# Pacing a spectral transform beside a feed-forward block: two straight lines for the transform's steps, and maxima of x taken five steps behind their loads

## The chip, the cores and the metric

The kernel runs on one core of one Trainium2 chip. The metric is the device time of one execution in microseconds (us), lower is better. The profile names the engines PE (TensorE, matmuls; PEld is its weight load), DVE (VectorE), ACT (ScalarE), POOL (GpSimd) and SP (SyncE, whose queue issues all DMA transfers here; SPq is that queue).

## The reference

For 8 batches of 3136 tokens with 256 channels: a filter in the frequency domain along the tokens, then a two-dimensional Fourier transform whose real part is added, a normalization over the channels, and a feed-forward block with 1024 hidden channels.

```python
X = np.fft.rfft(x, axis=1)
x = np.fft.irfft(X * (filt_r + 1j * filt_i)[None], n=3136, axis=1)
mixed = np.real(np.fft.fft(np.fft.fft(x, axis=1), axis=2))
u = x + mixed
mu = np.mean(u, axis=-1, keepdims=True)
var = np.mean((u - mu) ** 2, axis=-1, keepdims=True)
un = (u - mu) / np.sqrt(var + 1e-06)
out = u + np.maximum(un @ w_ch1, 0.0) @ w_ch2
```

## The kernel before

All matrix products run in float16, with each operand split into a high and a low part, so three matmuls stand for one. Two kinds of work share the engines.

**The transform of a batch, there and back.** `there(b)` is a generator; each `yield` ends one *step*, and a batch has `STEPS` = 63 of them.

- Stage 1 (`forward1`): seven loads of x (448 KB each, L379, tile `x`), one a step; `XLAG` steps behind each load the maximum of that tile on VectorE (`absmax`, L267, tile `mx`); then a scale `sx` from the seven maxima; then 14 steps, each with a cast on ScalarE and a subtraction on VectorE (L395), three matmuls (L400), an eviction by ScalarE and VectorE (L402, L403) and a store into the DRAM tile `d1` (224 KB, L404).
- Stage 2 (`forward2`): seven chunks. Each loads `at` from `d1` (L425), forms the spectrum (L449, L450), multiplies it by the filter on VectorE (L455, L459), finishes it on GpSimd, ScalarE and GpSimd or VectorE, and turns it around by a transposing DMA (`z`, L480). Two chunks later `inverse1` multiplies `z` (L514 to L516) and stores `bt` into the DRAM tile `d2` (L520). `fold` writes the chunk's even and odd parts into the ring `eo` of 1920 columns, from which the channel mix reads.
- The way back (`inverse2`, generator `back(b)`, 17 *back steps*): it loads `b` from `d2` (448 KB, L554; all chunks of `d2` have to be there), waits two more steps, forms y (L577), evicts it on ScalarE (`ys`, L584) and stores it into the DRAM tile `dy` (L560). The first back step of a batch holds its first b load, the fourth its first y product.

The generators begin a batch's transform when the one before is through its last step; a back step may come once all but the last step of its batch's transform are done.

**The feed-forward block.** Tokens go in 49 groups of 256 mirrored pairs of rows (two tiles of 128; 1568 pairs a batch, so group 6 holds the first pairs of batch 1, and groups 12, 18, 24, 30, 36 and 42 the first of batches 2 to 7). `fetch(g)` loads y from `dy` (L633); `prepare(g)` yields seven times: two channel mixes (L646, reading `eo`), the add on VectorE (L656), the statistics (L713, L714), the scale (L725 to L729), and two tiles that are normalized (L736), split (L739, L741) and turned around by a transposing DMA (`ut`, L746). Then the group has eight *products*: `first_product(g, f)` is six matmuls (L770) with an eviction in two halves (`h`: ScalarE L779, VectorE L780), and `second_product`, two products behind, is twelve matmuls into `acc` (L799). After the eighth, `acc` is added to y (L808) and stored (L811). 392 products make up the run.

**Pacing.** The main loop goes over the products q. In each it emits a first product, one yield of a group's preparation (group g+2 begins at f = 2 of group g), a second product, at most one back step, and then as many transform steps as a pacing line says. At f = 6 of group g, group g+3 is fetched, and `bring` emits at once whatever back steps its rows still need. For the first group with rows of batch 2 to 7 this is at q = 78, 126, 174, 222, 270 and 318. `advance` stops ahead of a fold whose ring columns have not been mixed yet:

```python
if s in folds and b * NS + folds[s] - RING > mixed[0]:
    return
```

The emitted order is not yet the order on the engines: a planner puts each engine's instructions in order by when it expects them to be ready, with priority by place in the program. `after("h")` and `after("pe")` keep an instruction behind the latest h eviction or first product on its engine.

Of the kernel before, what the change touches and what calls it, by code (L numbers as in the profile page):

```python
# [25 lines left out]
NS = N // 2  # L26
# [7 lines left out]


PAUSE = 4
XLAG = 3
FIRST = 21 + XLAG
STEPS = FIRST + PAUSE + 7 * 5
WAIT = 2  # L40
BACK = 1 + WAIT + 14
EARLY = 0.6
RISE = 28
SOON = 994
LOADED = 300
LOAD_AT = (19, 20, 21, 22, 50, 50, 54, 54)
LOAD_AFTER = (("d1", 10), ("d1", 11), ("d1", 12), ("d1", 13), ("bt", 3), ("bt", 3), ("bt", 4), ("bt", 4))
LOAD_IN = ("ut", "ut", "ys", "ys", "big", "big", "big", "big")
WIDEN_AT = (58, 59, 60, 61, 62, 63, 64, 65)
BOUND_AT = (62, 66)  # L50
SPLIT_AT = (63, 115)
FILTERS_AT = (2, 0, 1, 4, 6, 3, 8, 5)
FILTERS_ON_ACT = (0, 3, 4, 6)

# [134 lines left out]
def program(tc, a, NB):  # L189
    nc = tc.nc  # L190
    with ExitStack() as ctx:
        _program(ctx, tc, nc, a, NB)


def _program(ctx, tc, nc, a, NB):
# [18 lines left out]
    def after(*keys):  # L214

        order = ExitStack()
        for k in keys:
            if k in marks:
                order.enter_context(tc.issue_after(marks[k]))
        return order  # L220
# [45 lines left out]
    def absmax(dst, src, axis=AX.X):  # L266
        nc.vector.tensor_reduce(dst, src, axis=axis, op=ALU.max, apply_absolute_value=True)  # L267
# [104 lines left out]
    def forward1(b, d1):  # L372
        xs = [xp.tile([112, 4, 256], F32, tag="big", name=f"x_{b}_{q}") for q in range(7)]
        m = tp.tile([112, 8], F32, tag="mx", name=f"mx_{b}")
        for q in range(7 + XLAG):
            with after(("y", 1), ("un", 0)) if b == 1 else nullcontext():
                if q < 7:
                    with after("sp") if b > 1 else nullcontext():
                        nc.sync.dma_start(xs[q], a["x"][b, :, 4 * q : 4 * q + 4])  # L379
                if q >= XLAG:  # L380
                    with after("h"):
                        absmax(m[:, q - XLAG : q - XLAG + 1], xs[q - XLAG], AX.XY)
            if q < 6 + XLAG:
                yield
# [28 lines left out]
    def forward2(b, d1, d2):  # L413
# [109 lines left out]
        for c in range(far):  # L523
            load(c)
            if b:
                yield
        for _ in range(PAUSE - far if b else PAUSE + XLAG - 1):
            yield
# [96 lines left out]
    def fetch(g):  # L625
        y = ys_of[g] = mp.tile([128, 2, 2, 256], F32, tag="y", name=f"y_{g}", bufs=4)
        for t, (g0, g1) in enumerate(groups[g]):
            q = g0
            while q < g1:
                b = q // NS  # L630
                e = min(g1, (b + 1) * NS)
                with after(("un", 0)) if g == 2 else after(("out", g - 4)):
                    marks["y", g] = nc.sync.dma_start(  # L633
                        y[q - g0 : e - g0, t], dys[b][:, q - b * NS : e - b * NS].rearrange("k s c -> s k c")
                    ).ins
                q = e
# [119 lines left out]
    def first_product(g, f):  # L756
        y, ut = ready[g]
        m = groups[g][0][1] - groups[g][0][0]
        nt = 2 * sum(g1 - g0 for g0, g1 in groups[g])
        utv = ut[:, : len(groups[g])].rearrange("p t (k d l) q -> p t k d l q", k=2, d=2)  # L760
        p = ps_h.tile([128, 512], F32, tag="psh", name=f"h_{g}_{f}")
        even = nt == 2 * m * len(groups[g])
        runs = [(slice(0, len(groups[g])), 0, nt, m)] if even else [
            (slice(t, t + 1), 256 * t, 2 * (g1 - g0), g1 - g0) for t, (g0, g1) in enumerate(groups[g])
        ]
        for ts, c0, n, m in runs:
            i = 0
            for d in range(2):
                for hw, hx in ((0, 0), (0, 1), (1, 0)):
                    marks["pe"] = nc.tensor.matmul(  # L770
                        p[:, c0 : c0 + n].rearrange("p (t k q) -> p t k q", k=2, q=m),
                        w1s[:, d, hw, 128 * f : 128 * f + 128],
                        utv[:, ts, :, d, hx, :m],
                        start=i == 0,
                        stop=i == 5,
                    ).ins
                    i += 1
        h = mp.tile([128, 2, 512], F16, tag="h", name=f"h16_{g}_{f}", bufs=4)
        nc.scalar.activation(h[:, 0, :nt], p[:, :nt], AF.Relu)  # L779
        marks["h"] = nc.vector.scalar_tensor_tensor(  # L780
            h[:, 1, :nt], p[:, :nt], 0.0, h[:, 0, :nt], op0=ALU.max, op1=ALU.subtract
        ).ins
        hs[g, f] = h

    def second_product(g, f):
        tiles = groups[g]
        y = ready[g][0]
        h = hs.pop((g, f))
        if f == 0:
            accs[g] = [  # L790
                ps_o.tile([128, 2, 256], F32, tag="pso", name=f"acc_{g}_{t}") for t in range(len(tiles))
            ]
        c0 = 0
        for t, (g0, g1) in enumerate(tiles):
            m = g1 - g0
            acc = accs[g][t]
            for k in range(2):
                for i, (hh, hw) in enumerate(((0, 0), (0, 1), (1, 0))):
                    nc.tensor.matmul(  # L799
                        acc[:m, k],  # L800
                        h[:, hh, c0 : c0 + m],
                        w2s[:, f, hw],
                        start=f == 0 and k == 0 and i == 0,
                        stop=f == 7 and k == 1 and i == 2,
                    )
                c0 += m
            if f == 7:
                nc.vector.scalar_tensor_tensor(  # L808
                    y[:m, t], acc[:m], beta[:m], y[:m, t], op0=ALU.mult, op1=ALU.add
                )  # L810
                marks["sp"] = marks["out", g] = nc.sync.dma_start(a["out"][:, g0:g1].rearrange("k s c -> s k c"), y[:m, t]).ins  # L811
# [87 lines left out]
    def advance(n):  # L899

        while done[0] < min(n, NB * STEPS):
            b, s = divmod(done[0], STEPS)
            if s == 0 and come[0] < BACK * (b - 1) + 1:
# [3 lines that stand above are left out]
            next(forth)  # L907
            done[0] += 1

    def give(n):  # L910

        while come[0] < min(n, NB * BACK) and done[0] >= STEPS * (come[0] // BACK + 1) - 1:
            next(home)
            come[0] += 1
# [7 lines left out]
    def soon(slot):  # L922

        return max(need(slot), BACK * ((slot + LOADED) // NS) + 1 + WAIT)

    def bring(slot):
        advance(STEPS * (slot // NS + 1) - 1)
        give(need(slot))
        assert come[0] >= need(slot)

    todo = [(n, load_weights, i) for i, n in enumerate(LOAD_AT)]
    todo += [(n, widen_weights, i) for i, n in enumerate(WIDEN_AT)]
    todo += [(n, f, w) for f, at in ((bound_weights, BOUND_AT), (split_weights, SPLIT_AT)) for n, w in zip(at, ("w1", "w2"))]
    todo.sort(key=lambda t: t[0])
# [37 lines left out]
    work = prepare(1)  # L972
    for _ in range(AHEAD):
        next(work, None)
    per = NS // 32
    for q in range(8 * ng + LAG):
        g, f = divmod(q, 8)
        if g < ng:
            first_product(g, f)
        if f == 8 - AHEAD:  # L980
            for _ in work:
                pass
            if g + 2 < ng:
                work = prepare(g + 2)
        next(work, None)
        if q >= LAG:
            second_product(*divmod(q - LAG, 8))
        give(min(come[0] + 1, soon(32 * q + SOON)))
        advance(int(STEPS * (1 + min((q + 1) / RISE, (q + 1) / per + EARLY))))
        for ahead in [2] * (q == 0) + [g + 3] * (f == 6):  # L990
            if ahead < ng:
                bring(groups[ahead][-1][1] - 1)
                fetch(ahead)
# [54 lines left out]
```

## Time and profile before

| | |
|---|---|
| time, median of 3 runs | 1537.51 us (1533.45 to 1542.68) |
| the profiled execution | 1535.77 us, of which the span from the first to the last instruction is 1534.0 |
| mean granted TensorE clock | 0.955 |
| busy, share of the span | PE 91%, DVE 71%, ACT 50%, POOL 35% |
| moved by DMA | 268.98 MB, mean 175 GB/s |
| SyncE's 56 loads of x | 448 KB each |

Busy time is the union of an engine's instructions. The first eviction of a product starts at 149.0 us; before that, batch 0 is transformed alone.

### The profile page before, as it was taken

To read this page: it belongs to the slowest core of one execution; us is meant where nothing else is said; L and a number is where in the kernel's file an instruction comes from. 1 tells how busy PE (TensorE), PEld (TensorE's weight loads), DVE (VectorE), ACT (ScalarE), POOL (GpSimd) and SP (SyncE) were. 2 spreads that over 40 slices of the span, in tenths; PEclk is the share of its full clock that TensorE was granted. 3 is DMA by queue.
4 is the path that set the end of the run, shared out by engine and by line. 5 is a ranking of instruction groups with operands and counts; after the bars stand their busy time and mean duration, and the time that the engine had idled before them with its cause. 6 is when DMAs were issued, how large, how long until landed. Compare 5 with 4: busy or idle time off the path is not lost.

```text
span 1534.0 us, 30300 instructions
## 1 busy us (share of the span) xinstructions
PE 1398.7 (91%) x11331; PEld 934.1 (61%) x11331; DVE 1092.8 (71%) x2388; ACT 771.3 (50%) x1426; POOL 539.9 (35%) x682
## 2 busy tenths in 40 slices
PE   5454899787999999999999999899999999999998
PEld 1432567454665677566765677566665667666666
DVE  5576878586967887687758877688767877565562
ACT  4466545354545464474544654374644655443341
POOL 3652049205810195006720284016620284110110
PEclk8675999998999999999999999999999999999999
DMA  8868478959985797859986796859876896644320
GB/s 263 218 205 219 101 163 176 219 157 206 203 216 146 175 227 174 208 152 214 192 192 161 192 231 159 211 146 220 183 189 158 195 237 144 166 107 110 95 55 29
DMA packets 429491, 268.98 MB, mean 175 GB/s; under 512 B 218624, under 2 KB 395824, under 8 KB 429344
## 3 DMA queue, kind: packets, MB, share of 16 engines
q1 hardware_dynamic: 429344, 267.05, 72.5%
q8 instruction: 89, 1.46, 0.4%
q14 instruction: 58, 0.48, 0.1%
HBM read 113.36 MB, written 102.76 MB: 141 GB/s over the span
## 4 chain that ended last, share of the span: by engine, by line
PE 67%; DMA 11%; DVE 7%; issue 3%; POOL 3%; ACT 2%; SPq 1%; DVEq 0%; POOLq 0%; ACTq 0%
PE h L770 26%; PE acc L799 26%; DMA x<-x 3%; PE s L400 3%; PE y L577 3%; DMA at<-d 2%; PE mix L646 2%; DVE y L656 2%; PE i L514 1%; DMA b<-d 1%; PE i L516 1%; PE i L515 1%; PE s L449 1%; DVE mx L267 1%; PE s L450 1%
## 5 line engine op out<-in xcount | busy, mean ns | idle before, releaser
L770 PE MATMUL h<-ut,w1s 128*128 128x512 f16 x2352 | 590.8, 385 | 24.6 <-DVE h L780 20.5
L799 PE MATMUL acc<-w2s,h 128*128 128x256 f16 x4704 | 599.9, 274 | 1.3 <-DVE h L780 1.3
L799 PEld LDWEIGHTS <-h 128*128 128x128 f16 x4704 | 456.4, 98 | 146.8 <-issue 13.6
L779 ACT ACTIVATE h<-h 128x512 f16<-128x512 f32 x392 | 233.1, 595 | 411.9 <-PE h L770 404.6
L780 DVE SCALAR_TENSOR_TENSOR h<-h,h 128x512 f16<-128x512 f32 x392 | 267.6, 683 | 200.3 <-ACT h L779 199.3
L741 POOL TENSOR_TENSOR u<-un,u 128x512 f16<-128x512 f32 x94 | 107.8, 1163 | 758.0 <-ACT u L739 745.6
L770 PEld LDWEIGHTS <-w1s 128*128 128x128 f16 x2352 | 223.8, 99 | 236.7 <-issue 48.1
L656 DVE SCALAR_TENSOR_TENSOR y<-mix,alpha,y 128x508 f32<-128x508 f32 (+1 forms) x368 | 156.0, 474 | 8.2 <-PE mix L646 6.9
L736 ACT ACTIVATE un<-y,sb 128x256 f32<-128x256 f32 x196 | 101.8, 589 | 44.0 <-DVE sb L729 38.8
L469 POOL TENSOR_TENSOR y<-yt,y 128x448 f16<-128x448 f32 x105 | 108.4, 1036 | 16.5 <-ACT y L468 16.2
L584 ACT ACTIVATE ys<-y,alpha 128x512 f32<-128x512 f32 x112 | 76.1, 686 | 71.4 <-PE y L577 71.0
L519 DVE TENSOR_TENSOR bt<-i,bt 112x512 f16<-112x512 f32 x112 | 75.7, 682 | 49.1 <-ACT bt L518 47.4
L267 DVE TENSOR_REDUCE mx<-x 112x1 f32<-112x1024 f32 x56 | 67.7, 1214 | 52.0 <-DMA x<-x 52.0
L463 POOL TENSOR_TENSOR yt<-yt,t 128x224 f32<-128x224 f32 x112 | 73.9, 660 | 81.9 <-DVE t L459 53.6
L455 DVE SCALAR_TENSOR_TENSOR yt<-s,pF,ft 128x448 f32<-128x448 f32 x112 | 75.3, 675 | 37.7 <-PE s L450 34.9
L449 PE MATMUL s<-s,at 112*128 112x56 f16 x896 | 62.7, 191 | 32.6 <-DMA at<-d 28.1
L400 PE MATMUL s<-x,s 112*112 112x512 f16 x294 | 87.3, 388 | 3.9 <-ACT x L394 1.9
L577 PE MATMUL y<-b,i 112*64 112x512 f16 (+1 forms) x480 | 74.1, 396 | 18.1 <-DMA b<-d 17.9
L518 ACT CAST bt<-i 112x512 f16<-112x512 f32 x112 | 64.9, 585 | 49.9 <-PE i L516 43.7
L808 DVE SCALAR_TENSOR_TENSOR y<-acc,beta,y 128x512 f32<-128x512 f32 x98 | 71.2, 742 | 25.7 <-PE acc L799 25.5
L468 ACT CAST y<-yt 128x448 f16<-128x448 f32 x112 | 62.6, 564 | 38.6 <-POOL yt L464 35.6
L449 PEld LDWEIGHTS <-at 112*128 112x128 f16 x896 | 55.8, 98 | 42.6 <-DMA at<-d 36.0
(133 smaller groups left out, 1663.4 us busy)
## 6 DMA issues: line engine op xcount, KB each, us to landing
x<-x SPq DMA_DIRECT2D x56, 448.0 KB
d<-ast SPq DMA_DIRECT2D x112, 224.0 KB
at<-d SPq DMA_DIRECT2D x56, 448.0 KB
d<-bt SPq DMA_DIRECT2D x112, 224.0 KB
b<-d SPq DMA_DIRECT2D x56, 448.0 KB
out<-y SPq DMA_DIRECT2D x98, 256.0 KB
y<-dy SPq DMA_DIRECT2D x92, 256.0 KB
dy<-ys SPq DMA_DIRECT2D x208, 112.0 KB
```

The source lines that it names most:

```text
L267: nc.vector.tensor_reduce(dst, src, axis=axis, op=ALU.max, apply_absolute_value=True)
L400: nc.tensor.matmul(p, s1[:, hs], x16[:, hx], start=i == 0, stop=i == 2)
L449: nc.tensor.matmul(o, w, s2[:, U, 0].rearrange("p (r k) -> p r k", r=2), start=True, stop=False)
L469: last = half(b, hf == 1).tensor_tensor(ylo, ytv, yhi, op=ALU.subtract)
L577: nc.tensor.matmul(p[64 * h : 64 * h + 64, js], i2[:, t, h, i], bt[:, o + js.start : o + js.stop, h], start=i == 0, stop=i == 1,)
L656: nc.vector.scalar_tensor_tensor(out, p, al, y, op0=ALU.mult, op1=ALU.add)
L736: nc.scalar.activation(un[:m, k], y[:m, t, k], AF.Identity, bias=sb[:m, i, 1:2], scale=sb[:m, i, 3:4])
L741: marks["u16", g] = low.tensor_tensor(u16[:m, :, :, 1], unv, u16[:m, :, :, 0], op=ALU.subtract).ins
L770: marks["pe"] = nc.tensor.matmul(p[:, c0 : c0 + n].rearrange("p (t k q) -> p t k q", k=2, q=m), w1s[:, d, hw, 128 * f : 128 * f + 128], ut ...
L779: nc.scalar.activation(h[:, 0, :nt], p[:, :nt], AF.Relu)
L780: marks["h"] = nc.vector.scalar_tensor_tensor(h[:, 1, :nt], p[:, :nt], 0.0, h[:, 0, :nt], op0=ALU.max, op1=ALU.subtract).ins
L799: nc.tensor.matmul(acc[:m, k], h[:, hh, c0 : c0 + m], w2s[:, f, hw], start=f == 0 and k == 0 and i == 0, stop=f == 7 and k == 1 and i == 2,)
```

## The change

`XLAG` goes from 3 to 5, so a batch has 65 steps where it had 63, and the constants that count steps (`LOAD_AT`, `WIDEN_AT`, `BOUND_AT`, `SPLIT_AT`) move by two with it. The pacing line changes. With n = q + 1, the old one is the smaller of n/28 and n/49 + 0.6 batches beyond the first, which meet at n = 39.2. The new one is n/29 up to one batch at n = 29, and from there a straight line that reaches the end of the last batch at n = `last` = 8 x 39 + 4 = 316.

```diff
-XLAG = 3
+XLAG = 5
 FIRST = 21 + XLAG
 STEPS = FIRST + PAUSE + 7 * 5
...
-EARLY = 0.6
-RISE = 28
+RISE = 29
...
-LOAD_AT = (19, 20, 21, 22, 50, 50, 54, 54)
+LOAD_AT = (19, 20, 21, 22, 52, 52, 56, 56)
...
-WIDEN_AT = (58, 59, 60, 61, 62, 63, 64, 65)
-BOUND_AT = (62, 66)
-SPLIT_AT = (63, 115)
+WIDEN_AT = (60, 61, 62, 63, 64, 65, 66, 67)
+BOUND_AT = (64, 68)
+SPLIT_AT = (65, 115)
...
-    per = NS // 32
+    last = 8 * (NS * (NB - 1) // 256 - 3) + 4
...
-        advance(int(STEPS * (1 + min((q + 1) / RISE, (q + 1) / per + EARLY))))
+        n = q + 1
+        advance(int(STEPS * (1 + (n / RISE if n < RISE else 1 + (NB - 2) * (n - RISE) / (last - RISE)))))
```

## The prediction

> **What bounds the kernel now.** I read the page first, then busy time by stretch, then the waits of TensorE and VectorE, then single stretches of the timeline and the chain. The page gives the bound:
>
> ```profile
> span 1534.0 us, 30300 instructions
> ## 1 busy us (share of the span) xinstructions
> PE 1398.7 (91%) x11331; PEld 934.1 (61%) x11331; DVE 1092.8 (71%) x2388; ACT 771.3 (50%) x1426; POOL 539.9 (35%) x682
> ```
>
> TensorE is busy for 91% of the span, and the change adds and removes no matmul. What it can move is TensorE's idle time, so I looked for where that lies. Busy time by stretch (columns: stretch, its length, then busy time and instructions of each engine, granted TensorE clock, DMA share, GB/s):
>
> ```profile
> 250.00:300.00 50.00, 41.06 (x322) 28.26 (x321) 35.48 (x68) 22.67 (x44) 24.78 (x32) 0.97 0.80 184
> 300.00:350.00 50.00, 43.52 (x273) 25.08 (x272) 37.11 (x78) 26.67 (x48) 0.00 (x0) 0.93 0.60 175
> 350.00:400.00 50.00, 40.40 (x414) 27.87 (x415) 36.67 (x84) 23.43 (x46) 37.18 (x50) 0.86 0.98 213
> 450.00:1250.00 800.00, 776.42 (x6395) 518.41 (x6394) 614.29 (x1342) 421.75 (x780) 295.37 (x374) 0.99 0.80 188
> 1250.00:1500.00 250.00, 250.00 (x1928) 168.74 (x1926) 144.72 (x348) 109.17 (x203) 52.16 (x59) 1.00 0.50 120
> ```
>
> Three places follow. From 250 to 400 us TensorE is idle for 150 - 124.98 = 25.0 us: a knot. From 450 to 1250 us it is idle for 23.6 us, a thin loss. After 1250 us it is never idle, so nothing can be won there. TensorE's waits name the causes (total us, times, longest), first for 250 to 450 us:
>
> ```profile
> PE s L449 <- DMA at<-d: 10.4, 1, 10.4
> PE h L770 <- DVE h L780: 4.4, 4, 2.0
> PE h L770 <- DMA ut<-u: 3.2, 1, 3.2
> ```
>
> and for 450 to 1250 us:
>
> ```profile
> PE h L770 <- DVE h L780: 16.2, 8, 4.1
> PE s L449 <- DMA at<-d: 6.2, 8, 1.2
> ```
>
> The thin loss is mainly one thing: first products wait for VectorE's half of an older h (16.2 us). One of them, in VectorE's timeline,
>
> ```profile
> 983.17 1.22 DVE L267 TENSOR_REDUCE mx<-x 112x1 f32<-112x1024 f32 x1 [5.13 <-DMA x<-x]
> ```
>
> and in TensorE's,
>
> ```profile
> 986.60 2.72 PE L770 MATMUL h<-ut,w1s 128*128 128x512 f16 x6 [4.10 <-DVE h L780]
> ```
>
> with the total of VectorE's own waits for x after 250 us:
>
> ```profile
> DVE mx L267 <- DMA x<-x: 43.8, 21, 5.4
> ```
>
> VectorE stood 5.13 us in front of a maximum whose x had not landed; the h behind it came late, and TensorE stood 4.10 us.
>
> Pace is counted by the h evictions on ScalarE, one for each product. From 446 to 1316 us:
>
> ```profile
> L779 ACT ACTIVATE h<-h x245: 571/597/614, 448.3 to 1315.2; 128x512 f16<-128x512 f32 x123
> ```
>
> and from 259 to 446 us:
>
> ```profile
> L779 ACT ACTIVATE h<-h x41: 574/597/607, 266.2 to 444.4; 128x512 f16<-128x512 f32 x41
> ```
>
> So 870/245 = 3.55 us for a product in the long middle, but 187/41 = 4.56 in the knot: 187 - 41 x 3.55 = 41 us too many, of which part is transform steps that the old line does early and that are only moved.
>
> **The change, part by part.** With n = q + 1 products done, the old pace is 63(1 + min(n/28, n/49 + 0.6)) steps, which bends at n = 39.2; the new is 65(1 + n/29) up to n = 29 and then 65(2 + 6(n - 29)/287), since last = 8(42 - 3) + 4 = 316. From that I count by hand at which product each step is written:
>
> | batch | 2 | 3 | 4 | 5 | 6 | 7 |
> |---|---|---|---|---|---|---|
> | old: x first load / first maximum | 28/29 | 69/71 | 118/120 | 170/170 | 218/218 | 266/267 |
> | new | 29/33 | 77/81 | 125/129 | 173/176 | 221/224 | 268/272 |
> | old: first b load / first y product | 68/71 | 117/120 | 166/169 | 215/218 | 264/267 | 313/316 |
> | new | 77/78 | 124/126 | 172/174 | 220/222 | 268/270 | 316/318 |
> | first rows fetched, both | 78 | 126 | 174 | 222 | 270 | 318 |
>
> The zeros in the old rows come from the guard on the ring of 1920 columns: the last fold of batch 4 needs 4x1568 + 1568 - 1920 = 5920 mixed columns, which come at product 8x21 + 2 = 170, when the first half of group 23 is mixed, while the line asks for it at 166. When the guard opens, several steps come at once.
>
> *Maxima five steps behind.* No instruction is added; the loads and maxima of a batch are spread over two steps more. The lag grows from 0 to 2 products (0 to 7 us) to 3 or 4 (11 to 14 us). What a load takes, from the chain:
>
> ```profile
> 289.56 12.27 DMA b<-d
> ...
> 800.82 15.83 DMA x<-x
> ```
>
> and what stands ahead of the second in SyncE's queue:
>
> ```profile
> 797.21 3.09 SPq L379 DMA_DIRECT2D x<-x  x6
> ```
>
> The 15.83 us is the last of a burst of seven x loads, at the place where the guard had held batch 5. Spread at 65x6/287 = 1.36 steps a product, one x tile comes each 2.6 us, and 11 to 14 us cover it. By the Trainium skill (DMA: Bandwidth & Descriptors, Anatomy of one DMA) a transfer takes about 2.0 us plus its bytes over 436 GB/s, an estimate of 3.1 us for a 448 KB tile of x; by that rule the old lag would mostly do and the term would be near zero. Here the trace decides against it: a maximum waited 5.13 us and a load took 15.83.
>
> Bounds: nothing, or the whole 16.2 us and about 3 us of slow clock behind such gaps (the six matmuls at 986.60 took 2.72 us, where 1.46 is usual below). I take -13, near the upper end, since the row at 983.17 is the pattern. Its price: on SyncE the x loads keep their place behind the batch's first b load; on VectorE seven maxima move past two steps of other work, and it is busy for 614 of 800 us there; x is held two steps longer in buffers that the next tiles need only after stage 1. I take 0 for these.
>
> *The third batch slower.* Old, batch 2's loads are written at products 28 to 31 and its 14 stage-1 steps at 32 to 38, 2.25 a product; new, at 29 to 34 and 38 to 48, 1.36 a product. SyncE's queue in the knot, and VectorE's two costs of a stage-1 step:
>
> ```profile
> 286.62 2.90 SPq L379 DMA_DIRECT2D x<-x  x6
> 289.56 0.43 SPq L554 DMA_DIRECT2D b<-d  x1
> 291.84 7.17 SPq L560 DMA_DIRECT2D dy<-ys  x6
> ...
> 303.45 0.80 SPq L633 DMA_DIRECT2D y<-dy  x2
> ...
> 354.50 3.50 SPq L746 DMA_TRANSPOSE ut<-u  x1
> ```
>
> ```profile
> 322.83 0.68 DVE L403 TENSOR_TENSOR ast<-s,ast 112x512 f16<-112x512 f32 x1
> 323.43 0.74 DVE L395 SCALAR_TENSOR_TENSOR x<-x,sx,x 112x512 f16<-112x512 f32 x1
> ```
>
> Six x loads go out ahead of batch 1's second b load, which then takes 12.27 us; the dy stores and the fetch of group 6, which needs batch 1's first rows, stand behind. Then VectorE has 2.25 x 1.42 + 0.68 = 3.9 us of stage 1 and h for each product, more than the 3.55 a product may take, before any add of group 6; its second transpose goes out as late as 354.50, and product 48 waits for it. New: 1.36 x 1.42 + 0.68 = 2.6 us, and only the first x loads stand ahead of the stores. The 10.4 us at the first spectrum sit in the same hole. Batch 1 itself ends one product later (29 for 28, and its maxima two steps later): 3.6 us against the hole.
>
> Bounds: nothing, or all 41 us. I take -20: the idle time of the three stretches above the middle's rate, 25.0 - 3 x 50 x 23.6/800 = 20.6. The 12 or so steps put off run later inside TensorE's full time and cost what they cost before.
>
> *Back steps closer to the due time.* Between the last store of the transform and its batch's first y product lay 3 or 4 written products; now 2 (batch 2) or 3. What that chain takes, batch 3:
>
> ```profile
> 608.00 3.60 SPq L520 DMA_DIRECT2D d<-bt  x3
> 614.00 0.32 SPq L554 DMA_DIRECT2D b<-d  x1
> ```
>
> ```profile
> 618.72 0.63 PE L577 MATMUL y<-b,i 112*64 112x256 f16 x8
> ```
>
> From the end of the last store's issue to y: 7.1 us, 2 products, and the stores run one or two products behind where they are written. If TensorE took y where it is written, it would stand 5.4 us in batch 2 and some 3.3 in each of five others: 22 us. But list order is not engine order. The h evictions up to 290.4 us, and batch 1's first y product:
>
> ```profile
> L779 ACT ACTIVATE h<-h x38: 575/597/610, 149.0 to 288.4; 128x512 f16<-128x512 f32 x38
> ```
>
> ```profile
> 290.46 0.84 PE L577 MATMUL y<-b,i 112*64 112x256 f16 x10 [1.86 <-DMA b<-d]
> ```
>
> It is written at product 30 and stands after 38 products, where it waits 1.86 us: TensorE goes on with products until the planner takes b for landed. Bounds 0 and 22; I take +4, about twice that wait, as this row is the one with the shortest lead.
>
> Then the rows: from this y to the issue of the fetch at 303.45 it took 13 us in the worst case above, some 3.7 products; its flight I put at one of 5 us or so, as from b's issue at 614.00 to y at 618.72. Written, the add comes 6 products after the fetch, so y one product late still lands about when the add is due. The margin at the end of the line, group 24:
>
> ```profile
> 864.37 2.63 SPq L746 DMA_TRANSPOSE ut<-u  x2
> ```
>
> ```profile
> 872.24 1.46 PE L770 MATMUL h<-ut,w1s 128*128 128x512 f16 x6
> ```
>
> 5.2 us from the last issue to its use. Bounds 0 and 41 (below); I take +3, one product's lateness once.
>
> *Start and end.* Batch 0 gets two steps that issue nothing, and the weights' times move by the same two: 0. The transform ends at product 315 for 314, in full TensorE time: 0.
>
> Sum: -13 - 20 + 4 + 3 = -26, against the profiled execution's 1535.8 us (span 1534.0): **1510 us**. The median shown is 1537.5, 1.7 above that execution.
>
> **Rivals.** *The first rows of each batch come too late* (slower). Six groups (12, 18, 24, 30, 36, 42) begin with new rows; if each comes 12 us late, 5.2 are covered and TensorE stands 6.8 six times, 41 us: 1535.8 - 33 + 41 = 1544. It decides from 10.7 us of lateness each (33/6 + 5.2). For it: y moves 2 to 7 products toward the fetch while x loads, stores and ut transposes share SyncE's queue. Against: the 6 products between fetch and add. By the Trainium skill (the same page and section) the four hops (448, 112, 256 and 224 KB) sum to an estimate of some 10 us, three products, where two are left in batch 2; the trace's chain is longer still, and so it agrees with this rival's direction.
>
> *Only the maxima gain.* The knot is batch 1's lateness, now one product worse, and stays: 1535.8 - 13 + 4 = 1527. For it: batch 1's first y already stands 7 products behind its place. Against: the six x loads and 3.9 us of VectorE.
>
> *The waits only move.* The order on the engines is planned by readiness, the bend of the line is blurred by it, and the idle time returns elsewhere: 1536, give or take 6. For it: stage 1 of batch 2 was written from product 32, yet by the rows its steps still ran at 323 us, after more than 38 products. Against: 43.8 us of waits for x with a named cause.
>
> **How the numbers follow.** Forecast 0.55 (own range 1497 to 1523), only the maxima 0.16, waits move 0.16, late rows 0.13. About 0.5%, 8 us, is what a measurement of this kernel tells from no change: 1530 to 1545 is the same. Faster: 0.55 + 0.11 (most of the second) + 0.02 = 0.68; same: 0.05 + 0.13 + 0.02 = 0.20; slower 0.12. The range 1493 to 1538 leaves out the best end (the whole of both gains, 1535.8 - 19 - 41 = 1476) and most of the late rows.
>
> **What would show it.** Right: VectorE's wait for x falls from 43.8 to under 10 us, the 16.2 us of h waits to under 5; the knot's three stretches rise from 125 to at least 140 us of TensorE busy time; the b waits stay under 5. Wrong: a wait for ut at products 96, 144, 192, 240, 288, 336, or for b at a y product, of over 5 us each; or the hole before product 48 unchanged.

## The result, and the profile after

The changed kernel takes 1548.70 us (median of 6 runs, 1546.21 to 1552.16), the kernel before in the same session 1534.62: a ratio of 1.0086 [1.0059, 1.0113]. It is slower, by 14.1 us. The profiled execution took 1552.16 us, the longest of the six, of which the span is 1550.1. Its line numbers are one lower than before's, so L769 is the first product, L576 the y product, L448 the spectrum, L266 the maximum of x. In the experiments below, which keep before's numbers or add one, the tiles' names tell the groups.

The page of the changed kernel, its first rows:

```profile
span 1550.1 us, 30291 instructions
...
PE 1403.0 (91%) x11331; PEld 941.7 (61%) x11331; DVE 1106.1 (71%) x2388; ACT 768.3 (50%) x1426; POOL 540.2 (35%) x682
```

The span grew by 16.1 us, TensorE's busy time by 4.3 (1398.7 to 1403.0) for the same 11331 matmuls: they ran at a lower clock (0.951 for 0.955), which makes about a quarter of the difference between these two executions, idle time the rest. That the change lowers the clock is not shown: the six executions of the changed kernel had 0.951 to 0.957, and 27 of the kernel before in a later session 0.948 to 0.961. Busy time by stretch:

```profile
250.00:300.00 50.00, 41.98 (x367) 30.07 (x366) 40.51 (x73) 24.70 (x48) 34.52 (x45) 0.93 0.72 150
300.00:350.00 50.00, 39.06 (x246) 22.62 (x243) 29.06 (x62) 18.66 (x33) 2.43 (x2) 0.86 0.81 202
350.00:400.00 50.00, 46.86 (x386) 28.95 (x386) 39.13 (x89) 28.23 (x52) 9.58 (x12) 0.97 0.71 183
450.00:1250.00 800.00, 763.84 (x6228) 511.94 (x6226) 607.17 (x1316) 415.23 (x770) 275.20 (x345) 0.99 0.79 188
```

The knot (the first three rows) has 127.9 us of busy time, where before had 125.0 and at least 140 were expected: the hole has moved to 300 to 350 us and is hardly smaller. The long middle is worse: 36.2 us idle for 23.6. TensorE's waits in 450 to 1250 us, and under them VectorE's wait for x after 250 us:

```profile
PE y L576 <- DMA b<-d: 12.3, 7, 3.0
PE h L769 <- DVE h L779: 9.9, 7, 3.0
PE s L448 <- DMA at<-d: 9.7, 6, 4.2
PE i L513 <- DMA z<-y: 3.7, 3, 2.5
```

```profile
DVE mx L266 <- DMA x<-x: 23.2, 10, 5.1
```

The x waits did fall (43.8 to 23.2) and the h waits with them (16.2 to 9.9). In their place stand the waits for b (0.8 to 12.3), for `at` (6.2 to 9.7) and for z (0.4 to 3.7). Two of the b waits, on TensorE at batch 4's first y products, and SyncE's queue ahead of them:

```profile
819.01 1.06 PE L576 MATMUL y<-b,i 112*64 112x256 f16 x12 [1.58 <-DMA b<-d]
...
827.38 0.70 PE L576 MATMUL y<-b,i 112*64 112x512 f16 x4 [2.97 <-DMA b<-d]
```

```profile
809.07 1.79 SPq L519 DMA_DIRECT2D d<-bt  x3
814.22 0.32 SPq L553 DMA_DIRECT2D b<-d  x1
```

The last `bt` store is out at 810.86, b is asked for at 814.22, and y begins at 819.01 after a wait.

A second measure, used below, is the start of product k: of the six matmuls of the k-th `first_product`, counted from 0 in the timeline. Product 48 starts at 361.8 us before and 350.6 after, product 104 at 562.7 and 555.9, product 320 at 1326.1 and 1342.4; from there to the end both take the same time. Not all of a lead at product 48 is a gain, since the new line also puts transform work off. Products 320 to 391, with only the last batch's way back beside them, take 198.4 us, 2.79 each; the middle's 3.55 less that is 0.76 us of transform a product, an estimate of 37 us for a batch of 49 products. The new line stands 0.18 batch behind the old at n = 48 and 0.15 at n = 104, worth 6.7 and 5.7 us. So by this estimate only 4.5 of the lead of 11.2 us at product 48 are real, 1.1 are left at product 104, and from there to product 320, where the work put off is done, the change loses 17.4 us more than that work.

### The profile page after: what moved, and what is told of

Read it like the earlier page. It is cut to its first block, busy times and chain, and to the rows that moved or that the text cites. A ratio compares the mean times of both kernels' runs of the same rounds, so it can differ in the third digit from the quotient of the medians.

```text
span 1550.1 us, 30291 instructions
## 1 busy us (share of the span) xinstructions
PE 1403.0 (91%) x11331; PEld 941.7 (61%) x11331; DVE 1106.1 (71%) x2388; ACT 768.3 (50%) x1426; POOL 540.2 (35%) x682
## 4 chain that ended last, share of the span: by engine, by line
PE 60%; DMA 17%; DVE 10%; ACT 4%; POOL 3%; issue 3%; SPq 2%; DVEq 0%; ACTq 0%; POOLq 0%
PE h L769 24%; PE acc L798 22%; PE s L399 3%; DMA x<-x 3%; DMA b<-d 3%; PE y L576 3%; DMA at<-d 2%; DVE y L655 2%; PE mix L645 2%; DMA d<-bt 1%; DVE h L779 1%; DMA d<-ast 1%; PE i L513 1%; DMA ut<-u 1%; PE i L515 1%
## 5 line engine op out<-in xcount | busy, mean ns | idle before, releaser
L769 PE MATMUL h<-ut,w1s 128*128 128x512 f16 x2352 | 589.7, 384 | 22.4 <-DVE h L779 16.6
L769 PEld LDWEIGHTS <-w1s 128*128 128x128 f16 x2352 | 225.8, 99 | 238.2 <-issue 44.3
L468 POOL TENSOR_TENSOR y<-yt,y 128x448 f16<-128x448 f32 x105 | 108.7, 1039 | 24.1 <-ACT y L467 21.4
L462 POOL TENSOR_TENSOR yt<-yt,t 128x224 f32<-128x224 f32 x112 | 74.4, 665 | 94.7 <-DVE t L458 39.2
L576 PE MATMUL y<-b,i 112*64 112x512 f16 (+1 forms) x480 | 74.8, 407 | 29.1 <-DMA b<-d 29.0
L266 DVE TENSOR_REDUCE mx<-x 112x1 f32<-112x1024 f32 x56 | 67.3, 1212 | 30.8 <-DMA x<-x 30.5
L448 PE MATMUL s<-s,at 112*128 112x56 f16 x896 | 62.0, 192 | 28.1 <-DMA at<-d 23.0
L807 DVE SCALAR_TENSOR_TENSOR y<-acc,beta,y 128x512 f32<-128x512 f32 x98 | 71.2, 741 | 18.3 <-PE acc L798 18.2
L402 DVE TENSOR_TENSOR ast<-s,ast 112x512 f16<-112x512 f32 x98 | 66.6, 680 | 17.7 <-ACT ast L401 17.6
```

The costliest lines, as they stand in the source:

```text
L468: last = half(b, hf == 1).tensor_tensor(ylo, ytv, yhi, op=ALU.subtract)
L576: nc.tensor.matmul(p[64 * h : 64 * h + 64, js], i2[:, t, h, i], bt[:, o + js.start : o + js.stop, h], start=i == 0, stop=i == 1,)
L769: marks["pe"] = nc.tensor.matmul(p[:, c0 : c0 + n].rearrange("p (t k q) -> p t k q", k=2, q=m), w1s[:, d, hw, 128 * f : 128 * f + 128], ut ...
```

## The experiments

The first theory: two losses with a place. The lag of five makes batch 1 late, whose x landed long before, and eats the knot's gain; and the new line makes TensorE stand for b. The rival: every renumbering of the steps makes the planner deal the engines' orders anew, and the deals differ by as much as the effects looked for. All differences below are to the kernel before in the same session (1533.4 to 1535.65 us); the table at the end of this section holds them all.

**Each part alone.** First the lag of five on the old line.

```diff
-XLAG = 3
+XLAG = 5
...
-LOAD_AT = (19, 20, 21, 22, 50, 50, 54, 54)
+LOAD_AT = (19, 20, 21, 22, 52, 52, 56, 56)
...
-SPLIT_AT = (63, 115)
+SPLIT_AT = (65, 115)
```

> The five-step lag alone, on the old pacing line (before: 1534.6 us, after: 1548.7). Theory A (y products wait for b because the new line ends each batch 1 to 3 products before its rows are due, and the longer lag delays batch 1's stage 1): VectorE's waits for x after 250 us fall from 43.8 to under 20 us, TensorE's waits for b at y products after 450 us stay under 4, batch 1's stage 1 starts at 180 us or later instead of 172; time 1530 to 1541. Theory B (any renumbering of steps reshuffles the planner's order and costs or gains 1% at random): no relation to these waits, 1520 to 1555. Theory C (the transfers of x, b, dy and y bunch at the due time and slow one another): like before, 1530 to 1538, since the old line keeps them apart.

1526.15 us, 0.9941 [0.9922, 0.9960]: faster by 9.5 us. VectorE's wait for x after 250 us, TensorE's waits in 450 to 1250 us, and the busy row of that stretch:

```profile
DVE mx L267 <- DMA x<-x: 14.8, 8, 5.1
```

```profile
PE s L449 <- DMA at<-d: 12.0, 9, 3.1
PE h L770 <- DVE h L780: 2.9, 6, 0.9
```

```profile
450.00:1250.00 800.00, 782.09 (x6443) 524.38 (x6442) 624.11 (x1349) 425.94 (x791) 296.44 (x375) 0.99 0.82 190
```

The h waits fell from 16.2 to 2.9 us, as the prediction says. But the waits for `at` rose from 6.2 to 12.0, so the idle time fell by 5.7 us only, from 23.6 to 17.9.

Then the new line with the lag of three.

```diff
-RISE = 28
+RISE = 29
...
-    per = NS // 32
+    last = 8 * (NS * (NB - 1) // 256 - 3) + 4
...
-        advance(int(STEPS * (1 + min((q + 1) / RISE, (q + 1) / per + EARLY))))
+        advance(int(STEPS * (1 + ((q + 1) / RISE if q + 1 < RISE else 1 + (NB - 2) * (q + 1 - RISE) / (last - RISE)))))
```

> The new pacing line alone, with the lag of three steps. Theory A: TensorE's waits for b at y products after 450 us are 9 us or more (before 0.8, after 12.3); batch 1's stage 1 starts near 172 us, product 48 at 345 us or earlier (before 361.8, after 350.6); VectorE's waits for x after 250 us 30 us or more; time 1539 to 1548. Theory B: 1520 to 1555 without these marks. Theory C: b waits as in after, and 1545 to 1552.

1539.85 us, 1.0029 [1.0015, 1.0042]: slower by 4.2 us. Busy time by stretch, and the waits in 450 to 1250 us:

```profile
250.00:300.00 50.00, 45.20 (x377) 31.51 (x375) 31.17 (x60) 23.88 (x46) 20.74 (x26) 1.00 0.86 189
300.00:350.00 50.00, 45.77 (x290) 27.70 (x287) 42.50 (x91) 27.31 (x49) 2.28 (x2) 0.97 0.66 183
350.00:400.00 50.00, 44.65 (x440) 30.19 (x439) 39.68 (x97) 24.46 (x47) 30.13 (x39) 0.93 0.94 210
450.00:1250.00 800.00, 760.12 (x6258) 508.14 (x6256) 610.57 (x1313) 415.46 (x770) 287.13 (x362) 0.99 0.78 188
```

```profile
PE h L770 <- DVE h L780: 12.4, 14, 2.4
PE s L449 <- DMA at<-d: 11.8, 8, 3.4
PE y L577 <- DMA b<-d: 10.9, 8, 2.7
```

Here the knot did open: 135.6 us of busy time for 125.0, and product 48 starts at 328.6, 33.2 us sooner, 26.5 of them real. But at product 104 only 12.5 are left, and at product 320 the kernel is 0.7 us behind. The middle is idle for 39.9 us.

The parts alone add to -9.5 + 4.2 = -5.3; together they make +14.1. Some 19 us are their interaction.

**Batch 1's lag.** The changed kernel, with batch 1's maxima three steps behind their loads and the two steps it saves left empty ahead of its stage 2, so that all later numbering stays.

```diff
-        for q in range(7 + XLAG):
+        lag = 3 if b == 1 else XLAG
+        for q in range(7 + lag):
...
-        for _ in range(PAUSE - far if b else PAUSE + XLAG - 1):
+        for _ in range(PAUSE - far + (XLAG - 3 if b == 1 else 0) if b else PAUSE + XLAG - 1):
```

> The changed kernel, but batch 1 keeps its maxima three steps behind (its two spare steps stand empty ahead of stage 2). Theory A: batch 1's stage 1 starts near 172 us instead of 183.6, product 48 comes 5 to 10 us earlier than after's 350.6, the b waits stay at 10 to 14 us; time 1539 to 1544. Theory B: no relation, 1535 to 1560. Theory C: 1546 to 1550, since nothing at the due times changes.

1535.57 us, 1.0004 [0.9986, 1.0022]: 14.2 us of the loss gone. Batch 1's first stage-1 product and its first y, and the stretch of 325 to 350 us, first in the changed kernel:

```profile
183.56 0.38 PE L399 MATMUL s<-x,s 112*112 112x512 f16 x1
306.22 1.06 PE L576 MATMUL y<-b,i 112*64 112x256 f16 x12
```

```profile
325.00:350.00 25.00, 16.68 (x77) 8.72 (x75) 19.38 (x50) 10.99 (x20) 2.43 (x2) 0.73 0.75 179
```

then with batch 1 at a lag of three:

```profile
172.95 0.38 PE L401 MATMUL s<-x,s 112*112 112x512 f16 x1 [2.17 <-ACT x L395]
286.62 1.06 PE L578 MATMUL y<-b,i 112*64 112x256 f16 x12 [0.23 <-DMA b<-d]
```

```profile
325.00:350.00 25.00, 25.00 (x165) 15.24 (x163) 22.57 (x44) 17.91 (x32) 2.27 (x2) 1.00 0.59 168
```

And in the kernel before, batch 1's x loads in SyncE's queue and its first maximum in VectorE's timeline:

```profile
122.59 5.95 SPq L379 DMA_DIRECT2D x<-x  x7
```

```profile
151.61 1.21 DVE L267 TENSOR_REDUCE mx<-x 112x1 f32<-112x1024 f32 x1
```

The maximum runs 23 us after the last load was issued and waits for nothing; in batch 1 the lag had nothing to win. Its two steps put stage 1 off by 10.6 us and batch 1's first y by 19.6. Group 6 needs those rows, and TensorE, full at a clock of 1.00 without the delay, has 16.68 busy us at 0.73 with it. Product 48 starts at 333.4 for 350.6. The chain of work that ends with it in the changed kernel shows where the time went (parts of it):

```profile
299.06 2.57 DMA d<-bt
...
316.14 6.04 DMA y<-dy
...
322.20 9.28 DMA x<-x
...
331.50 1.22 DVE mx L266
...
346.82 3.72 DMA ut<-u
...
350.58 1.47 PE h L769 x6
```

It leads from batch 1's last `bt` store to the fetch of its rows. Then VectorE stands before a maximum of batch 2, whose x takes 9.28 us to land among those transfers, before it gets to the next adds. In the knot a lag of five does not cover the load: 11.0 of the 23.2 us of waits for x lie before 450 us.

The same edit on the old line with the lag of five:

> The lag of five steps on the old line, but three in batch 1. Theory A: on the old line the knot is held by batch 2's early stage 1 and not by batch 1's lateness, so product 48 stays near 359 us and the time near the lag alone, 1523 to 1529; with the new line the same edit was worth 13 us. If batch 1's lag costs the same everywhere: 1513 to 1518. Theory B: 1520 to 1550.

1531.73 us, 0.9977 [0.9957, 0.9997], 6.9 us less gain than with five everywhere. On the old line product 48 starts late in both (359.1 and 365.3 us): there batch 1's delay isn't what the knot waits for. So the delay in batch 1 costs 14.2 us on the new line and goes with a gain of 6.9 on the old, 21 us between them. The 6.9 us alone prove little: one product's shift of the old line costs more (below).

**The waits for b.** The changed kernel, with the first b load of batches 2 to 7 taken from the `d2` of the batch before, which has long been there. The first 224 pairs of those batches then get wrong rows; the transfers and matmuls are the same.

```diff
-        d2v = d2.rearrange("(m r) j l c -> (r j l) m c", r=2)
+        d2v = d2.rearrange("(m r) j l c -> (r j l) m c", r=2); d2p = d2s[max(b - 1, 0)].rearrange("(m r) j l c -> (r j l) m c", r=2)
...
-                bts[c].rearrange("p j h c -> p (j h) c"), d2v[:, 8 * c : 8 * c + 8]
+                bts[c].rearrange("p j h c -> p (j h) c"), (d2p if c == 0 and b > 1 else d2v)[:, 8 * c : 8 * c + 8]
```

> The changed kernel, but for batches 2 to 7 the first b load reads the same rows of the batch before, which have long been stored: the output of the first 224 pairs of those batches is wrong, the transfers and matmuls are the same, and the first y product no longer waits for the transform's last store. Theory A: TensorE's waits for b after 450 us fall from 12.3 to under 5, time 8 to 12 us lower, 1537 to 1541. Theory C: the bunch stays, and so does the time, 1546 to 1551. Theory B: 1535 to 1560.

1535.59 us, 1.0004 [0.9987, 1.0020]: 14.2 us gone as well, with this busy row in the middle:

```profile
450.00:1250.00 800.00, 776.30 (x6377) 518.65 (x6375) 617.68 (x1339) 420.01 (x785) 284.23 (x358) 0.99 0.79 190
```

Idle time 23.7 us, 12.5 less than in the changed kernel, and no wait for b: the wait of 12.3 us was worth its size there. Both cures at once:

> The changed kernel with both single cures at once: batch 1's maxima three steps behind, and the first b load of batches 2 to 7 taken from the batch before (its first 224 pairs then use wrong data). Each alone took 13 us off. Theory A (two separate losses, batch 1 late and TensorE standing for b): they add, 1548.7 - 26 = 1523 us (1519 to 1527), no wait for b at a y product after 450 us, and product 48 begins by 336 us. Theory B (each edit only deals the planned order anew, with a scatter of some 10 us, and the changed kernel was a bad deal): the second cure adds little, 1530 to 1540 us.

1524.97 us, 0.9934 [0.9913, 0.9955]: the second cure brought another 9.8 us (10.4 us of b waits stood in the kernel it was added to). They add nearly in full, as the theory of two losses asks. On the new line with the lag of three the same cure should have done as much:

> The new line alone with the first b load of batches 2 to 7 taken from the batch before (its first 224 pairs then use wrong data). The line alone stood 10.9 us for b after 450 us and took 1540 us. Theory A: the knot's gain then shows, 1527 to 1531 us, and no wait for b. Theory B: the time falls by less than 5 us, 1535 to 1540, as other waits take the place.

1539.55 us, 1.0037 [1.0016, 1.0057]: nothing. TensorE's waits in 450 to 1250 us:

```profile
PE h L770 <- DVE h L780: 10.5, 11, 1.8
PE s L449 <- DMA at<-d: 10.3, 7, 2.8
PE i L514 <- DMA z<-y: 9.8, 6, 2.4
```

The 10.9 us for b are gone, and z has 9.8 where it had 0.4; the idle time is 37.0 us for 39.9. What the b wait is worth depends on what is late behind it, and here the theory of two losses missed.

**The line's end.** If b is late because the steps end late, an earlier end should heal it. The end at 308 for 316:

```diff
-    last = 8 * (NS * (NB - 1) // 256 - 3) + 4
+    last = 308
```

> The changed kernel with the second line ending at product 308 instead of 316: the last store of batches 2 to 7 is written 4 or 5 products ahead of the first y product instead of 2 or 3, all real data and real waits. Theory A (y waits for b are what the line's end costs): waits for b after 450 us from 12.3 to under 4 us; time 8 to 12 us below after's 1548.7, 1537 to 1541; the knot as in after, product 48 near 350 us. Theory B (any renumbering reshuffles): 1525 to 1555 without these marks. Theory C (traffic bunched at the due time): a gain too, but the b waits stay above 6 us while VectorE's waits for x fall below after's 23.

1543.39 us, 1.0058 [1.0035, 1.0081]. And with the edit for batch 1 from above as well, at `last` = 308, 312 and 300:

> The line that ends at 308 together with three steps of lag in batch 1 and five elsewhere. Theory A, in which the two losses lie at different places and add up: product 48 near 333 us as with the lag of three in batch 1 alone, b waits after 450 us under 4; time 1521 to 1529, below both kernels and below the lag alone (1526.2) if the knot's gain stays. Theory B: 1525 to 1550, no sum of the parts.

1528.02 us, 0.9962 [0.9941, 0.9982].

> The changed kernel with batch 1's maxima three steps behind, and the line's end at product 312: half way between 316 (1535.6 us) and 308 (1528.0 us). Theory A (steps that end too late): 1530 to 1534 us, and the waits for b after 450 us between 9 and 11 us. Theory B (a new deal for each numbering): off that line by over 4 us, as likely above 1536 as below 1528.

1527.26 us, 0.9959 [0.9938, 0.9980].

> The same with the line's end at product 300. Theory A: the gain goes on but flattens, since the guard on the ring holds the folds of the later batches back: 1521 to 1528 us, waits for b after 450 us under 5 us. Theory B: no relation to the dose, 1525 to 1540 us. If the knot comes back, since batch 2 then has 45 products for 48, product 48 begins later than 340 us and the time rises to 1530 or more.

1562.77 us, 1.0175 [1.0142, 1.0209]. The line alone, with the lag of three, to 308:

> The new line with the lag of three, its end at product 308. Theory A: what stood late for b and z comes 2 to 8 products earlier, 1529 to 1534 us, and the waits for x (40.6 us with the end at 316) stay over 30 us. Theory B: within 4 us of the line alone, 1536 to 1544 us.

1531.32 us, 0.9977 [0.9958, 0.9996]. Against the same kernel with the end at 316, an end at 308 gains 5.1, 6.3 and 6.3 us and one at 312 gains 6.1: as much for four products as for eight, and then 29 us are lost at 300. Nor is it the b waits that go. With the end at 312, the waits in 450 to 1250 us begin

```profile
PE y L578 <- DMA b<-d: 14.9, 7, 3.9
PE s L450 <- DMA at<-d: 10.0, 7, 3.5
```

with more for b than at 316 (10.4), while h fell from 8.5 to 1.3. At 300 they begin

```profile
PE i L515 <- DMA z<-y: 11.8, 3, 7.8
PE s L450 <- DMA at<-d: 11.1, 7, 2.9
PE h L771 <- DVE h L781: 10.6, 8, 2.4
```

and product 320 starts 24.8 us later than at 316. So an end 4 or 8 products earlier helped in all four pairs, but hardly through b, whose waits fell by 3.1, 0.9 and 1.7 us at 308 and rose at 312. Nor is it a rule: an end at 300 loses, and one product later gains 3.0 us too (below). Why 300 is so bad is open. Counted from the source, the guard on the ring lets 18 steps out at once at product 266 there, 8 with the end at 308, 3 at 312, and behind product 40 never more than 2 at 316. That fits, but no run takes the guard away.

**One product's shift.** What does a renumbering cost that no named mechanism should feel? The old line, one product earlier (`EARLY` 0.62 for 0.6) and one later (0.58), with the lag of three:

```diff
-EARLY = 0.6
+EARLY = 0.62
```

> A scale for theory B: the kernel before with its second line 0.02 batches higher, so that the transform runs about one product earlier from product 41 on and nothing else is changed. Theory A: none of its waits change by more than 3 us in total; 1532 to 1540. Theory B: a step of 8 us or more up or down from 1535.6.

1544.62 us, 1.0064 [1.0040, 1.0088]. And with `EARLY = 0.58`:

> The kernel before with its line one product later (EARLY 0.58), the shift to the other side of the one that cost 10 us. Theory A with a smooth dependence: the line is at its best near 0.6 or the way down goes on, 1530 to 1540 us. Theory B: the old line at 0.6 is one of its better deals, 1538 to 1546 us here too.

1548.00 us, 1.0076 [1.0049, 1.0102], with this row for the middle:

```profile
450.00:1250.00 800.00, 762.46 (x6237) 508.41 (x6236) 599.13 (x1308) 411.84 (x763) 277.52 (x351) 0.99 0.78 184
```

One product to either side costs 10.2 and 14.6 us. The middle's idle time, 37.5 us here and 30.6 at 0.62, is near what the new line has (36.2 in the changed kernel); before's 23.6 is the least of the three. The same two shifts with the lag of five:

> The lag of five on the old line, moved one product earlier (EARLY 0.62): the same small shift that cost the kernel before 10 us. Theory A (the lag takes away the waits for x whatever the numbering): the waits for x after 250 us stay under 20 us, and the time is 1526, give or take 4. Theory B: the shift costs here too, or anything between 1524 and 1540; above 1532 would say that the lag's 9.5 us were within the scatter of the deal.

1535.98 us, 1.0006 [0.9988, 1.0025], and

> The old line one product later (EARLY 0.58) with the lag of five. With the lag of three this numbering took 1548.0 us, and VectorE waited 53.5 us for x. Theory A (the lag takes the waits for x away in every numbering): waits for x under 20 us and a gain of 8 us or more, 1534 to 1540 us. Theory B (each numbering is a new deal): any time from 1525 to 1550, with no fixed gain.

1543.01 us, 1.0062 [1.0036, 1.0089]. Numbering by numbering the lag of five is worth 9.1, 9.5 and 5.0 us (0.62, 0.6, 0.58), and its mark is there each time: x waits 43.0 to 20.0, 43.8 to 14.8, 53.5 to 14.8 us. The expectation for 0.62 had named a time above 1532 us as the sign that the lag's gain is scatter. The time is above it, and yet at the same numbering the gain stands. The numbering is worth more than the lag, with either lag (10.2 and 14.6 us with three, 10.7 and 19.1 with five): it is no noise of the run but a property of the emitted order. The changed kernel with `last` = 317:

> The changed kernel with the new line's end one product later (last = 317 for 316), which no mechanism named so far should feel by more than a product at the very end. Theory A: 1546 to 1552 us, the waits for b after 450 us again 10 to 14 us, batch 1's stage 1 again from about 183 us. Theory B: the time moves by over 5 us either way, most likely down (1535 to 1543), as the old line moved by 10 us for one product.

1545.95 us, 1.0070 [1.0044, 1.0096]; the new line is less touchy there, 3.0 us. Last, the lag of four on the old line:

```diff
-XLAG = 3
+XLAG = 4
...
-SPLIT_AT = (63, 115)
+SPLIT_AT = (64, 115)
```

> The maxima four steps behind their loads on the old line. Theory A: between three (1534.6 us, waits for x 43.8 us) and five (1526.2 us, 14.8 us): 1528 to 1533 us, waits for x 20 to 35 us. Theory B: outside, 1535 to 1545 us, as a shift of the numbering may cost 10 us by itself.

1536.89 us, 1.0024 [1.0001, 1.0046], outside three and five. Its waits for x lie between theirs, 27.7 us, and those for h fell to 5.8, but for `at` TensorE now stands 15.3 us in the middle and 9.3 in the knot, and product 48 starts at 366.1 us, the latest of all.

All runs together. The last four columns are of one profiled execution each, which lies up to 7.0 us from its kernel's median, so differences of a few us between two of their rows mean little.

| kernel | us | to before | x waits | middle idle | product 48 | product 320 |
|---|---|---|---|---|---|---|
| before | 1534.6 | | 43.8 | 23.6 | 361.8 | 1326.1 |
| changed | 1548.7 | +14.1 | 23.2 | 36.2 | 350.6 | 1342.4 |
| lag 5 alone | 1526.2 | -9.5 | 14.8 | 17.9 | 359.1 | 1317.8 |
| line alone | 1539.9 | +4.2 | 40.6 | 39.9 | 328.6 | 1326.8 |
| changed, batch 1 lag 3 | 1535.6 | -0.1 | 22.6 | 32.7 | 333.4 | 1323.2 |
| lag 5 alone, batch 1 lag 3 | 1531.7 | -2.7 | 14.6 | 18.2 | 365.3 | 1324.0 |
| changed, b cured | 1535.6 | -0.1 | 16.8 | 23.7 | 351.6 | 1328.3 |
| changed, both cures | 1525.0 | -9.9 | 15.3 | 21.4 | 330.5 | 1310.1 |
| line alone, b cured | 1539.6 | +4.7 | 28.8 | 37.0 | 331.3 | 1328.0 |
| changed, end 308 | 1543.4 | +9.0 | 15.4 | 27.1 | 347.2 | 1326.6 |
| end 308, batch 1 lag 3 | 1528.0 | -6.4 | 17.8 | 28.1 | 334.7 | 1320.4 |
| end 312, batch 1 lag 3 | 1527.3 | -6.2 | 15.9 | 28.4 | 331.7 | 1317.1 |
| end 300, batch 1 lag 3 | 1562.8 | +29.3 | 28.0 | 47.8 | 330.9 | 1348.0 |
| line alone, end 308 | 1531.3 | -2.1 | 30.8 | 29.8 | 324.8 | 1323.7 |
| changed, end 317 | 1546.0 | +11.1 | 29.3 | 33.2 | 349.2 | 1335.1 |
| old line 0.62 | 1544.6 | +10.2 | 43.0 | 30.6 | 364.4 | 1336.7 |
| old line 0.58 | 1548.0 | +14.6 | 53.5 | 37.5 | 355.7 | 1341.7 |
| lag 5, old line 0.62 | 1536.0 | +1.2 | 20.0 | 18.6 | 359.5 | 1324.0 |
| lag 5, old line 0.58 | 1543.0 | +9.6 | 14.8 | 24.8 | 358.7 | 1330.3 |
| lag 4 alone | 1536.9 | +3.5 | 27.7 | 23.2 | 366.1 | 1332.2 |

Of the versions that load each batch's own b, the lag of five alone is the fastest, at 1526.15 us, and the new line to 312 with batch 1 at a lag of three is next, at 1527.26: both beat the kernel before and the changed one, and between the two nothing is decided. Of the eighteen times expected under Theory A, four came true: the line alone, the line alone to 308, the end at 308 with batch 1 at a lag of three, and both cures.

## Why the prediction was wrong

Forecast 1510 us, measured 1548.7: 39 us apart, and on the other side of no change. Three steps failed above all: the price of the lag in batch 1, the cost of the work that the new line puts off, and the place at which the first y products run. Step by step:

- **The bound and the three places** were read rightly. Of the 16.1 us between the two profiled executions 11.8 are idle time of TensorE: the middle has 12.6 more, the knot 2.9 less.
- **Maxima five steps behind, -13.** The mechanism is shown, in three numberings, but the size was over-read: 9.5, 9.1 and 5.0 us. With the lag alone 13.3 us of the h waits did go, yet the term took TensorE's idle time to fall by as much; 5.8 us of waits for `at` took their place, and the middle's idle time fell by 5.7. The trace decided against the Trainium skill's rule here (DMA: Bandwidth & Descriptors, Anatomy of one DMA), by which the term would have been near zero, and the runs agree with the trace. That section is on transfers which GpSimd issues, while here SyncE's queue issues them.
- **The price of that lag in batch 1, booked as one product, 3.6 us.** This step failed. "Its maxima two steps later" was counted as steps, yet the two steps come before stage 1 and everything of batch 1 follows them: stage 1 stands 10.6 us later and the first y 19.6, and the loss is 14.2 us (15.4 and 9.8 in the two other pairs on the new line). The lag was taken as one edit for all batches, though batch 1's maxima, at 151.61 us and on, had no x to wait for.
- **The third batch slower, -20.** As to the knot, and for the line alone, this was right: 26.5 us of lead at product 48, the work put off taken away. The failure is the sentence behind it, that the steps put off run later "inside TensorE's full time and cost what they cost before". They ran in a middle that was not full: from product 48 to 320 the line alone gave all of it back.
- **Back steps closer, +4 between 0 and 22.** The failed step is "list order is not engine order". In the changed kernel the first y products of batches 3 to 7 stand at products 126, 174, 222, 270 and 318, the very ones at which they are written, and batch 2's two behind its 78; TensorE took them there and stood for b, 12.3 us in the middle. The value was taken from batch 1's y, which stood seven products behind its place because its b was late, not because the planner moves such work. The hand count of 22 was the nearer bound, and the cure was worth 14.2 and 9.8 us, though nothing on the line alone.
- **First rows late, +3, and the rival that ended slower.** There was no wait for `ut` after 450 us. The kernel is slower for other reasons than the one that rival named; that its 1544 us came near is chance.
- **The sum.** Adding the terms was itself a step, and it failed: 19 us lie in the interaction. "The waits only move" was the rival nearest to the truth, and its 6 us to either side were too few: a shift of one product moved the time by 3.0 to 19.1.

That first y products run where they are written could be read from the kernel before. Batch 3's is written at product 120, that is behind 121 products (the count begins at 0), and starts at 618.72 us. The h evictions up to there, and in the changed kernel, where it is written at 126, up to 639.8 us:

```profile
L779 ACT ACTIVATE h<-h x121: 572/597/610, 149.0 to 618.4; 128x512 f16<-128x512 f32 x121
```

```profile
L778 ACT ACTIVATE h<-h x127: 569/597/607, 151.1 to 635.8; 128x512 f16<-128x512 f32 x127
```

The counts are 121 and 127, the written places, and in the kernel before the same holds for batches 2 and 4 to 7. The prediction rested on batch 1, the one that differs.

What is shown, then: on the new line batch 1's lag costs 14.2 us, and 9.8 and 15.4 in two more pairs (with b cured, and with the end at 308), each time with product 48 starting 12.5 us later or more. The waits for b cost 14.2 us in the changed kernel and 9.8 with batch 1 cured, where the middle's idle time fell by 12.5 and 11.3. Both together make 24. For b the case is weaker: that edit also tells the planner of other ready times, so the order may be dealt anew, and in a third kernel it gained nothing. What stays open is why the line alone loses its lead in the middle. Its idle time there, 39.9 us, isn't tied to one wait: taking b away brought z. The old line has as much when it is shifted by one product (37.5 us), so the new line need have no fault of its own; it may only lack what the old one has at 0.6 and at no neighbour tried. A lag of five lowers the middle's idle time on the old line in every numbering (30.6 to 18.6, 23.6 to 17.9, 37.5 to 24.8 us).

## What to carry to other kernels

Where a planner orders the engines from an emitted order, measure what a shift by one product costs before pricing an edit that renumbers the steps: here it was 10 and 15 us, more than either part of the change alone, and the kernel before was the best of the three tried. A delay that helps where data are late hurts where they have long landed, so apply a lag batch by batch and ask which chain the batch ends in. A lead at an early product is a gain only less the work put off, and only if it still stands where the work is done.

## What the runs showed of the hardware

TensorE's granted clock fell here after waits of 2 to 3 us. In the changed kernel the wait of 2.97 us that ends at 827.38 is followed by a stretch granted 0.60, and two stretches later the clock is full again:

```profile
823.00:827.00 4.00, 1.41 (x10) 0.83 (x9) 1.82 (x2) 2.64 (x6) 2.23 (x2) 1.00 1.09 265
827.00:831.00 4.00, 3.62 (x15) 1.18 (x15) 0.00 (x0) 1.37 (x2) 0.04 (x1) 0.60 0.84 217
831.00:835.00 4.00, 4.00 (x32) 2.62 (x31) 2.20 (x3) 1.05 (x3) 0.00 (x0) 0.97 1.09 255
835.00:839.00 4.00, 4.00 (x41) 2.90 (x39) 3.62 (x6) 1.03 (x2) 0.00 (x0) 1.00 0.93 236
```

So a wait of 2.97 us cost, by estimate, about 4.00 x 0.40 = 1.6 us more in slow matmuls. A wait of 1.93 us, for `at` at 725.11 in the same kernel, went the same way, with 0.57 granted behind it:

```profile
721.00:725.00 4.00, 1.99 (x40) 1.38 (x37) 4.00 (x10) 0.60 (x1) 0.00 (x0) 1.00 1.17 245
725.00:729.00 4.00, 3.89 (x28) 2.25 (x29) 2.85 (x9) 0.00 (x0) 2.45 (x4) 0.57 1.18 241
```

Not every wait does it: behind the 1.58 us at 819.01 the clock stayed at 1.00. By the Trainium skill (TensorE: Matmul & The Clock Gate, Part 1: The HAM clock gate) the clock falls after an idle window of about 3.4 us and comes back after about as long a busy one; the way back agrees, while the falls came here after gaps of 2.97 and 1.93. Between the profiled executions of the changed kernel and the one with both cures, of 32.3 us of span 9.0 are busy time (1403.0 and 1394.0 us for the same matmuls). These were a long and a short execution of their kernels, whose medians are 23.7 us apart, so part of that is scatter; but waits cost their length and then some of the clock.
